# Attention values kept as two fp16 parts instead of three bf16 parts and one fp16 part

## The chip, the cores and the metric

The kernel runs on one core of one Trainium2 chip. A core has five engines that run beside each other: TensorE (PE, matrix products; its weight loads are listed apart as PEld), VectorE (DVE), ScalarE (ACT), GpSimd (POOL) and SyncE (SP), which here only issues DMAs. Products land in PSUM, 8 banks of 128 x 512 fp32; everything else works from SBUF. The metric is the time of one execution on the device, in microseconds; lower is better. The kernel was timed in three runs.

## The reference

A modulated layer norm, attention with 32 heads of 16 columns over 2048 rows of 512, and then a mixing block with its own layer norms, four weight matrices and two gelus. Everything is fp32 and a single sequence.

```python
h = _layernorm(x) * (1 + ca) + sa
q, k, v = split(h @ wqkv)                       # 32 heads x 16
scores = einsum("bhqd,bhkd->bhqk", q, k) * 16 ** -0.5
p = softmax(scores)
x = x + ga * (einsum("bhqk,bhkd->bhqd", p, v) @ wo)
h = _layernorm(x) * (1 + cb) + sb
x1 = h + shift(gelu(_layernorm(h) @ w1)) @ w2
x = x + gb * (x1 + gelu(_layernorm(x1) @ w3) @ w4)
```

## The kernel before

**Precision.** PE works on numbers with short mantissas, so each fp32 matrix is split into a high and a low part and a product is made of three (helper `mm3`, lines 339, 341 and 343, which every projection uses). The probabilities P are kept as integers: the exponential (line 1017) writes int32, scaled by 2^26. The upper 16 bits of each integer are read in place as fp16 numbers; the lower 16 bits are turned into fp16 by `p_low` (lines 1057 to 1073), on POOL as a rule (L1072) and in two halves on ACT when POOL lags (it shows as L127 in the profile). v is kept so that P times v keeps its digits: three bf16 parts of 16 columns each (offsets 0, VD = 20 and 2 VD = 40 of the 64 columns that belong to a head), a column of ones beside the first part, which yields the softmax's denominator, and a fourth copy in fp16, scaled down by VHI, for the lower halves of P. A tile row of v has 192 two-byte numbers for two heads: 128 for the three parts (`v_hi`), 64 for the fp16 copy (`v_lo`). `v_weights` scales each column of v's weights by a bound on that column, so that v stays under VMAX; the scale is put back in wo.

**Making v.** `v_tiles` runs over 16 row tiles for each half of the heads, 32 tiles in all. A tile is 12 matmuls into a bank, then a chain: ACT copies the first part (L770), ACT the fp16 copy (L771), DVE subtracts the first part from the bank into an fp32 tile vr (L751), ACT copies the second part from vr (L773), POOL subtracts that from vr for the third part (L774), and a store to DRAM follows (Vs). At most three tiles are alive (`vlive`) and at most two use vr (`vrs`). For the first half the part that unit 0 needs also goes straight to the tile vst.

**Attention.** A unit is two heads and a chunk of 512 queries; there are 64 units of 16 steps (a step s is 128 keys), 1024 steps in all. For each step PE makes two score blocks (L1021), ACT their exponentials (L1017), POOL the lower halves (L1072), and PE the products with v: `pv_part` has four matmuls for the upper halves (L1098, 32 columns of v each, two for each head) and, once for two steps, four and four for the lower halves (L1095). All of them add up in one bank. Row maxima are taken 24 steps ahead: PE makes the scores the other way round (L1005), DVE reduces them (L1001), and the shift goes into the query tile through small DMAs. At a unit's end ACT copies the bank (`ac_copy`), PE transposes it (L1127), DVE sums the parts (L1134, `sums`), takes the reciprocal of the denominator (L1144), and POOL multiplies (L1138, `fin`).

**Order.** All engines' queues are written in advance by a planner in the kernel (`Sched`). It keeps a modelled time for each engine; attention is the main line and everything else is filler, dealt out between its blocks by a budget. `sch.chain` queues the steps of a chain with a modelled cost each; `sch.dma` (line 101) charges each DMA to a modelled SP queue, with its bytes divided by 360 per ns and at least 475 ns. Its count of bytes per element is line 103:

```python
n = 2 if o.dtype == BF16 else 4
```

Filler in time order: v for heads 0 to 15, keys, v for heads 16 to 31, keys, queries, meanwhile the splitting of the other weights into 40 half pieces (`pieces_load`, `pieces_gen`; loads to the tiles wst, results stored to Ws by way of three tiles wq). The rest of the network for a chunk of 512 rows is `tail(ci)`; its weights come back from Ws. The first tail may start once all keys, values, queries and pieces are done, at step 248 at the earliest (constant TPO); from step 264 on (TPL) the program waits for them by force. The last tail runs after attention has ended.

Of the kernel before, what the change touches and what calls it, by code (L numbers as in the profile page):

```python
# [8 lines left out]
F32 = mybir.dt.float32  # L9
F32R = mybir.dt.float32r  # L10
BF16 = mybir.dt.bfloat16
F16 = mybir.dt.float16
I32 = mybir.dt.int32
U16 = mybir.dt.uint16
AF = mybir.ActivationFunctionType
OP = mybir.AluOpType
AX = mybir.AxisListType
# [3 lines left out]
S, D, H, DH, F = 2048, 512, 32, 16, 1792  # L21
P = 128
KT = D // P
NKT = S // P
# [6 lines left out]
GELU_C = 0.7978845608028654  # L31
PBITS = 26
PEXP = PBITS * 0.6931471805599453
VHI = 2.0 ** 39
VMAX = 2.0 ** 14
VD = 20

SC0 = (32, 900.0, 700.0)
TAILB = (0.0, 500.0, 560.0, 590.0)
# [24 lines left out]
NV = 3  # L64
# [233 lines left out]
def cA(n=CH):  # L298
    return n / 1.2 + 52
# [6 lines left out]
def cG(n=CH):  # L306
    return 2.2 * n + 40
# [3 lines left out]
def kernel(ctx, tc, A_x, A_wqkv, A_wo, B_w1, B_w2, B_w3, B_w4, c, w_mod, out):  # L311
# [46 lines left out]
        return t[:, :, 0:128].rearrange("p a (b n) -> p a b n", b=2)  # L358

    def v_lo(t):  # L360
        return t[:, :, 128:192].bitcast(F16).rearrange("p a (b n) -> p a b n", b=2)


    ident = con.tile([P, P], F32, name="ident")
# [13 lines left out]

    Qs = dr.tile([H * DH, 3, S], F32, name="Qs")
    Ks = dr.tile([H * DH, 3, S], F32, name="Ks")  # L380
    Vs = dr.tile([NP, P, NKT, 192], BF16, name="Vs")
    FG = [(0, 4), (4, 4), (8, 4), (12, 2)]
    pieces = []
    order = {"wo": [], "w1": [], "w2": [], "w3": [], "w4": []}
# [88 lines left out]

    kst, qtl = [], []

    zero = con.tile([4, CH], F32, name="zero")
    pool.memset(zero, 0.0)

    def unit_tiles(pl, i, e, e2):
# [234 lines left out]

    vt = []
    for i in range(NV):
        t = qp.tile([P, H // 4, 192], BF16, name=f"vt{i}")
        pool.memset(t, 0.0)
        pool.memset(v_hi(t)[:, :, :, DH:DH + 1], VHI)
        pool.memset(v_lo(t)[:, :, :, 8 + DH:9 + DH], 1.0)  # L720
        vt.append(t)

    def v_gen(w, a):
# [2 lines left out]
        yield lambda: not vlive  # L726
        done.add(("v", a))

    vlive, vrs = [], [0]
    direct, near = [], set()  # L730

    def v_tiles(w, a, kts):
        wh, wl = halves(w, KT)
        for kt in kts:
            ci, t = divmod(kt, TPC)
            h = hT[ci]
            yield lambda: len(vlive) < NV and vrs[0] < 2 and sch.room() and ("hT", ci) in done
            vrs[0] += 1
            vlive.append(kt)
            b = dbank("v")[:, :256]  # L740
            for k in range(KT):
                for _ in mm3(b, h[:, k, 0, t * P:(t + 1) * P], h[:, k, 1, t * P:(t + 1) * P],
                             wh[:, k], wl[:, k], k == 0, k == KT - 1):
                    yield nsq(256)
            w = vt[kt % NV]
            v, vl = v_hi(w), v_lo(w)
            b3 = b.rearrange("p (a b d) -> p a b d", b=2, d=DH)
            r = qp.tile([P, H // 4, 2, DH], F32, name="vr", tag="vr", bufs=2)

            def rest(v=v, b3=b3, r=r, b=b):  # L750
                dve.tensor_tensor(r, b3, v[:, :, :, 0:DH], op=OP.subtract)  # L751
                sch.free(b)

            def store(kt=kt, w=w):
                vrs[0] -= 1

                if not a and direct:
                    sch.dma(dma.dma_start, direct[kt // 4][:, kt % 4], w[:, 0])
                    near.add(kt)

                def gone():
                    vlive.remove(kt)
                    done.add(("vk", a, kt))
                    if kt % 4 == 3:
                        done.add(("v", a, kt // 4))
                e = sch.dma(dma.dma_start, Vs[8 * a:8 * a + 8, :, kt, :].rearrange("a p n -> p a n"),
                            w)
                sch.after(e, gone)

            sch.chain(("A", cA(256), lambda v=v, b3=b3: act.activation(v[:, :, :, 0:DH], b3, AF.Copy)),  # L770
                      ("A", cA(256), lambda vl=vl, b3=b3: act.activation(vl[:, :, :, 8:8 + DH], b3, AF.Copy, scale=1.0 / VHI)),  # L771
                      ("D", cD(256), rest),
                      ("A", cA(256), lambda v=v, r=r: act.activation(v[:, :, :, VD:VD + DH], r, AF.Copy)),  # L773
                      ("G", cG(256), lambda v=v, r=r: pool.tensor_tensor(v[:, :, :, 2 * VD:2 * VD + DH], r, v[:, :, :, VD:VD + DH],  # L774
                                                                         op=OP.subtract)),
                      (None, 0, store), prio=VP, bank=b)

    def v_weights(a):
# [175 lines left out]

    unit_tiles(at, 1, pool, pool)
    qst, mxs, osb = {}, {}, {}
    vst = [at.tile([P, NKT // 4, 192], BF16, name=f"vst{i}") for i in range(4)]
    direct += vst
    pv, pt = {}, {}
    pts = [at.tile([P, 2, CH], I32, name=f"pt{i}") for i in range(NPT)]  # L960
# [1 line left out]
    def load_unit(u):  # L962
        ci, pr = units[u]
        qst[u] = q = qtl[u % 3]
        cs = slice(ci * CH, (ci + 1) * CH)
        load_rows(q, Qs, pr, cs, slice(0, CH))
        if u > 2:
            sch.dma(dma.dma_start, q[0::32].bitcast(F32), zero)
        load_rows(kst[u % 3], Ks, pr, slice(0, S), slice(0, S))

    vnext = set()
# [85 lines left out]
    def p_low(s):  # L1057

        p = pt[s].rearrange("p j n -> p (j n)")
        o, i = p.bitcast(F16)[:, 0::2], p.bitcast(U16)[:, 0::2]  # L1060
        ready = e_exp.pop(s) + XX
        g, a = [max(sch.T[e], ready) for e in "GA"]
        if g > a + LACT:

            def half(h):
                c = slice(h * CH, (h + 1) * CH)
                e_low[s] = XP["A"] + sch.crit("A", 690, ready, partial(act.activation, o[:, c], i[:, c], AF.Copy, scale=0.5))
            half(0)
            e_low[s] += 690 + 480
            second.append(partial(half, 1))  # L1070
        else:
            e_low[s] = XP["G"] + sch.crit("G", 1345, ready, lambda: pool.tensor_scalar(  # L1072
                o, i, 0.5, 1.0, op0=OP.mult, op1=OP.mult))

    def pv_ready(s, lo):

# [2 lines left out]
    def pv_part(s, lo):  # L1079


        u, kt = divmod(s, NKT)
        if kt == 0 and not lo:
            pv[u] = ap_.tile([P, CH], F32, name="pv", tag="v", bufs=1)
        load_v(u, kt // 4) if (u, kt // 4) in vnext else None
        v, acc = vst[kt // 4], pv[u]

        def mms():
            for j in range(2):
                for i in range(2):  # L1090
                    r = 64 * j + 32 * i
                    if lo:
                        n = 9 + DH if i else 1 + DH
                        c = 128 + 32 * j + 9 + DH
                        te.matmul(acc[r:r + n, :], v[:, (kt + i) % 4, c - n:c].bitcast(F16), pt[s + i].bitcast(F16)[:, j, 0::2],  # L1095
                                  start=False, stop=kt == NKT - 2, skip_group_check=True)
                    else:
                        te.matmul(acc[r:r + 32, :], v[:, kt % 4, r:r + 32], pt[s].bitcast(F16)[:, j, 1::2],  # L1098
                                  start=kt == 0, stop=False, skip_group_check=True)
        e = sch.put("P", CCOL, 0.0, mms)  # L1100
        if lo:
            for i in range(2):
                pts.append(pt.pop(s + i))
                e_low.pop(s + i)
            if kt % 4 == 2:
                if u + 1 < NU:
                    vnext.add((u + 1, kt // 4))
                sch.after(e + VLATE, partial(load_v, u + 1, kt // 4))
            if kt == NKT - 2:
                acs.append((u, e + COUT))  # L1110
# [9 lines left out]
    def o_fin(u, ac, ready):  # L1120
        ci, pr = units[u]
        if pr == 0:
            osb[ci] = at.tile([P, TPC, D], F32, name="osb", tag="osb", bufs=1)
        yield lambda: sch.T["P"] >= ready and sch.room()
        b = dbank("ot")
        for t in range(TPC):
            te.transpose(b[:, t * P:(t + 1) * P], ac[:, t * P:(t + 1) * P], ident)  # L1127
            yield 110
        bv = b.rearrange("p (th n) -> p th n", n=64)
        sm = at.tile([P, 8, DH + 1], F32, name="sm", tag="sm", bufs=1)  # L1130
        rc = at.tile([P, 8, 1], F32, name="rc", tag="rc", bufs=2)

        def sums():
            dve.reduce_sum(sm, bv[:, :, 0:3 * VD].rearrange("p th (a d) -> p th d a", a=3)[:, :, 0:DH + 1, :], axis=AX.X)  # L1134
            sch.free(b)

        def fin():
            pool.tensor_tensor(osb[ci][:, :, pr * 32:pr * 32 + 32].rearrange("p t (h d) -> p t h d", d=DH),  # L1138
                              sm[:, :, 0:DH].rearrange("p (t h) d -> p t h d", h=2),
                              rc.rearrange("p (t h) o -> p t h o", h=2).to_broadcast([P, TPC, 2, DH]), op=OP.mult)  # L1140
            if pr == NP - 5:
                sch.add(tail(ci), 0 if ci == NC - 1 else None)

        sch.chain(("D", 490, sums), ("D", 90, lambda: dve.reciprocal(rc, sm[:, :, DH:DH + 1])), ("G", 350, fin),  # L1144
                  *([mark(("att", ci))] if pr == NP - 1 else []), prio=0, bank=b)


# [555 lines left out]
```

## Time and profile before

| what | us |
|---|---|
| median of 3 runs | 1999.7 |
| the runs | 1993.77, 1999.7, 2000.05 |
| span of the profiled execution (the page gives no other time of it) | 2000.7 |
| PE busy in it | 1920.9 |
| DVE, ACT, POOL busy | 1652.2, 1473.6, 1676.1 |
| first score matmuls of attention, last product with v | about 98, 1846 |

Each engine's row on the page gives busy time, share of the span and instructions. A group of instructions is named by line, engine, operation, output <- input, shapes and count; behind the first bar stand total busy us and mean ns, behind the second the idle time of the engine just before and what ended it. Rows that begin with a stretch (206.00:330.00) give an engine's busy time in it, with the number of its instructions. A wait "A <- B: 91.4, 221, 3.8" says that A waited for B for 91.4 us in all, 221 times, 3.8 us at the longest.

### The profile page before, as it was taken

Reading aid. Unit: us, or ns where it says so; the run is one execution under the profiler, and the core shown is the slowest. Engines: PE = TensorE matmul, PEld = TensorE weight load, DVE = VectorE, ACT = ScalarE, POOL = GpSimd, SP = SyncE. Lnnn points to the kernel's source line nnn. Section 1 sums busy time; section 2 is a strip of 40 time slices with the busy share of each in tenths; the row PEclk is TensorE's granted clock in tenths of the full one; section 3 lists DMA queues with packets and bytes.
Section 4 is the critical chain, followed back from the end, with each engine's and each line's share of the span. In section 5 each row is a group of like instructions: output and inputs, shape, how many; then the busy total and the mean of one; then the engine's idle time right before and its main releaser. Section 6 shows DMA issues by size and latency. Waiting matters only on the chain.

```text
span 2000.7 us, 42354 instructions
## 1 busy us (share of the span) xinstructions
PE 1920.9 (96%) x14480; PEld 1146.7 (57%) x14480; DVE 1652.2 (83%) x3010; ACT 1473.6 (74%) x3083; POOL 1676.1 (84%) x1609
## 2 busy tenths in 40 slices
PE   7999999999999999999999999999999999999899
PEld 4655555555455555555455555555555555555798
DVE  7887988888899888888989898898898889883643
ACT  5376888777878777777878787786787878777443
POOL 6287999889999998888999998898899989888532
PEclk8999999999999999999999999999999999999999
DMA  5767677766643334345433333334433343334432
GB/s 184 205 201 228 182 231 218 244 225 192 198 157 111 115 103 143 109 136 162 126 111 92 109 111 114 115 119 148 157 98 100 115 151 107 121 95 147 149 146 90
DMA packets 232352, 293.24 MB, mean 147 GB/s; under 512 B 125876, under 2 KB 177076, under 8 KB 215848
## 3 DMA queue, kind: packets, MB, share of 16 engines
q1 hardware_dynamic: 232136, 290.53, 46.4%
q8 instruction: 115, 1.88, 0.4%
q14 instruction: 101, 0.83, 0.1%
HBM read 225.81 MB, written 62.91 MB: 144 GB/s over the span
## 4 chain that ended last, share of the span: by engine, by line
PE 67%; DVE 16%; ACT 8%; issue 3%; POOL 2%; DMA 2%; SPq 1%; POOLq 0%; ACTq 0%; DVEq 0%
PE mb L1005 14%; PE sc L1021 10%; PE pv L1098 10%; DVE mx L1001 9%; PE w L339 7%; PE w L343 6%; PE w L341 6%; PE pv L1095 4%; ACT pt L1017 4%; POOL pt L1072 2%; DVE xs L1421 1%; DVE sq L1418 1%; DMA vst<-Vs 1%; PE mr L644 1%; PE ot L1127 1%
## 5 line engine op out<-in xcount | busy, mean ns | idle before, releaser
L1072 POOL TENSOR_SCALAR pt<-pt 128x1024 f16<-128x1024 uint16 x988 | 1312.5, 1365 | 132.6 <-ACT pt L1017 125.4
L1001 DVE TENSOR_REDUCE mx<-mb 128x1 f32<-128x512 f32 x2048 | 1281.0, 683 | 76.0 <-PE mb L1005 54.5
L1017 ACT ACTIVATE pt<-sc 128x512 int32<-128x512 f32 x2048 | 1090.8, 606 | 272.3 <-PE mb L1005 164.9
L1005 PE MATMUL mb<-kst,qtl 64*128 64x512 f32 x2048 | 752.1, 454 | 49.0 <-ACT pt L1017 16.1
L1021 PE MATMUL sc<-qtl,kst 64*128 64x512 f32 x2048 | 716.4, 444 | 2.6 <-DVE A L329 0.6
L1005 PEld LDWEIGHTS mb<-kst,qtl 64*128 64x128 f32 x2048 | 348.7, 193 | 254.5 <-DVE mx L1001 91.4
L1021 PEld LDWEIGHTS sc<-qtl,kst 64*128 64x128 f32 x2048 | 335.6, 186 | 153.5 <-DVE mx L1001 47.1
L1098 PE MATMUL pv<-pt,vst 128*32 128x512 f16 x4096 | 358.2, 397 | 0.1
L1095 PE MATMUL pv<-pt,vst 128*17 128x512 f16 (+1 forms) x2048 | 213.7, 394 | 2.2 <-POOL pt L1072 1.7
L1098 PEld LDWEIGHTS <-vst 128*32 128x32 bf16 x4096 | 90.9, 95 | 167.6 <-issue 108.8
L339 PE MATMUL w<-A,wr 128*128 128x256 f32 (+2 forms) x576 | 175.3, 304 | 0.3 <-ACT A L333 0.3
L1428 POOL TENSOR_TENSOR g<-xs,g 128x256 fp32r<-128x256 f32 (+2 forms) x144 | 103.2, 718 | 83.4 <-ACT g L1427 81.3
L341 PE MATMUL w<-A,wr 128*128 128x256 f32 (+2 forms) x576 | 169.8, 295 | 0.5 <-DVE A L329 0.3
L343 PE MATMUL w<-A,wr 128*128 128x256 f32 (+2 forms) x576 | 167.7, 291 | 0.0
L339 PEld LDWEIGHTS w<-A,wr 128*128 128x128 f32 x576 | 109.6, 190 | 35.4 <-DVE mx L1001 10.3
L339 PE MATMUL w<-wr,g 128*128 128x512 f32 x288 | 119.2, 414 | 0.6 <-ACT g L1427 0.6
L341 PEld LDWEIGHTS w<-A,wr 128*128 128x128 f32 x576 | 109.9, 191 | 12.4 <-issue 11.3
L343 PE MATMUL w<-wr,g 128*128 128x512 f32 x288 | 114.7, 398 | 0.2 <-POOL g L1428 0.2
L341 PE MATMUL w<-wr,g 128*128 128x512 f32 x288 | 113.6, 394 | 0.0
L343 PEld LDWEIGHTS w<-A,wr 128*128 128x128 f32 x576 | 109.8, 191 | 6.7 <-issue 6.7
L1535 DVE TENSOR_TENSOR x<-x,w 128x512 f32<-128x512 f32 x64 | 43.9, 687 | 82.0 <-PE w L343 82.0
L1424 ACT ACTIVATE sq<-w 128x256 f32<-128x256 f32 (+2 forms) x144 | 55.7, 387 | 68.8 <-PE w L343 66.0
(151 smaller groups left out, 2103.8 us busy)
## 6 DMA issues: line engine op xcount, KB each, us to landing
wr<-Ws SPq DMA_DIRECT2D x80, 1024.0 KB
kst<-Ks SPq DMA_DIRECT2D x189, 256.0 KB
vst<-Vs SPq DMA_DIRECT2D x252, 192.0 KB
qtl<-Qs SPq DMA_DIRECT2D x192, 64.0 KB
Vs<-vt SPq DMA_DIRECT2D x32, 384.0 KB
Ws<-wq SPq DMA_DIRECT2D x40, 256.0 KB
Ws<-wst SPq DMA_DIRECT2D x40, 256.0 KB
wst<-in_B_w_dram SPq DMA_DIRECT2D x36, 256.0 KB
```

The costliest lines, as they stand in the source:

```text
L339: te.matmul(o, lh, rh, start=first, stop=False)
L341: te.matmul(o, lh, rl, start=False, stop=False)
L343: te.matmul(o, ll, rh, start=False, stop=last)
L1001: end = sch.crit("D", 605, e + PX, lambda: dve.reduce_max(mxs[u][:, j, g, c:c + 1], b, axis=AX.X))
L1005: return ready, lambda: te.matmul(b, lhs, kst[u % 3][r, c * CH:(c + 1) * CH], start=True, stop=True), after
L1017: ea = sch.crit("A", 480, e + PX, lambda: act.activation(pt[s][:, j], b, AF.Exp))
L1021: return ready, lambda: te.matmul(b, kst[u % 3][r, kt * P:(kt + 1) * P], qst[u][r], start=True, stop=True), after
L1072: e_low[s] = XP["G"] + sch.crit("G", 1345, ready, lambda: pool.tensor_scalar(o, i, 0.5, 1.0, op0=OP.mult, op1=OP.mult))
L1095: te.matmul(acc[r:r + n, :], v[:, (kt + i) % 4, c - n:c].bitcast(F16), pt[s + i].bitcast(F16)[:, j, 0::2], start=False, stop=kt == NKT - 2 ...
L1098: te.matmul(acc[r:r + 32, :], v[:, kt % 4, r:r + 32], pt[s].bitcast(F16)[:, j, 1::2], start=kt == 0, stop=False, skip_group_check=True)
L1424: sch.chain(("A", cA(n), lambda: act.activation(sq, b, AF.Square)), ("D", cD(n), cube), ("A", cA(n), lambda: act.activation(sq, sq, AF.Tan ...
L1428: ("G", cG(n), lambda: pool.tensor_tensor(lo, xs, hi, op=OP.subtract)), (None, 0, end), bank=b)
```

## The change

v is kept as two fp16 parts (offsets 0 and VD = 32) with the column of ones scaled to 2^15, and one further fp16 copy of the first part scaled by 2^-20, for the lower halves of P, which are scaled by 2^-20 instead of 0.5. The second part is written by the DVE subtraction itself; the fp32 tile vr, the second ACT copy and the POOL subtraction are gone, and with them the limit of two tiles on vr. The lower halves' matmuls all have 17 columns (before, 17 and 25). The sum at a unit's end runs over two parts, its planned cost is 360 ns instead of 490, and its tiles have two and three buffers instead of one and two. The tile of zeros is 4 x 128 instead of 4 x 512 and is read four times over by the DMA. The tiles of v are of type F16 instead of BF16; line 103 is as it was.

```diff
-VHI = 2.0 ** 39
-VMAX = 2.0 ** 14
-VD = 20
+VHI = 2.0 ** 15
+VMAX = 1.0
+VLO = 2.0 ** -20
+PLO = 2.0 ** -20
+VD = 32
...
-        return t[:, :, 128:192].bitcast(F16).rearrange("p a (b n) -> p a b n", b=2)
+        return t[:, :, 128:192].rearrange("p a (b n) -> p a b n", b=2)
...
-    Vs = dr.tile([NP, P, NKT, 192], BF16, name="Vs")
+    Vs = dr.tile([NP, P, NKT, 192], F16, name="Vs")
...
-    zero = con.tile([4, CH], F32, name="zero")
+    zero = con.tile([4, P], F32, name="zero")
...
-        t = qp.tile([P, H // 4, 192], BF16, name=f"vt{i}")
+        t = qp.tile([P, H // 4, 192], F16, name=f"vt{i}")
         pool.memset(t, 0.0)
         pool.memset(v_hi(t)[:, :, :, DH:DH + 1], VHI)
-        pool.memset(v_lo(t)[:, :, :, 8 + DH:9 + DH], 1.0)
+        pool.memset(v_lo(t)[:, :, :, DH:DH + 1], VHI * VLO)
...
-            yield lambda: len(vlive) < NV and vrs[0] < 2 and sch.room() and ("hT", ci) in done
-            vrs[0] += 1
+            yield lambda: len(vlive) < NV and sch.room() and ("hT", ci) in done
...
-                dve.tensor_tensor(r, b3, v[:, :, :, 0:DH], op=OP.subtract)
+                dve.tensor_tensor(v[:, :, :, VD:VD + DH], b3, v[:, :, :, 0:DH], op=OP.subtract)
...
-                      ("A", cA(256), lambda vl=vl, b3=b3: act.activation(vl[:, :, :, 8:8 + DH], b3, AF.Copy, scale=1.0 / VHI)),
+                      ("A", cA(256), lambda vl=vl, b3=b3: act.activation(vl[:, :, :, 0:DH], b3, AF.Copy, scale=VLO)),
                       ("D", cD(256), rest),
-                      ("A", cA(256), lambda v=v, r=r: act.activation(v[:, :, :, VD:VD + DH], r, AF.Copy)),
-                      ("G", cG(256), lambda v=v, r=r: pool.tensor_tensor(v[:, :, :, 2 * VD:2 * VD + DH], r, v[:, :, :, VD:VD + DH],
-                                                                         op=OP.subtract)),
...
-    vst = [at.tile([P, NKT // 4, 192], BF16, name=f"vst{i}") for i in range(4)]
+    vst = [at.tile([P, NKT // 4, 192], F16, name=f"vst{i}") for i in range(4)]
...
-            sch.dma(dma.dma_start, q[0::32].bitcast(F32), zero)
+            sch.dma(dma.dma_start, q[0::32].bitcast(F32).rearrange("r (a n) -> r a n", n=P),
+                    zero[:, None, :].to_broadcast([4, CH // P, P]))
...
-                o, i, 0.5, 1.0, op0=OP.mult, op1=OP.mult))
+                o, i, PLO, 1.0, op0=OP.mult, op1=OP.mult))
...
-                        n = 9 + DH if i else 1 + DH
-                        c = 128 + 32 * j + 9 + DH
-                        te.matmul(acc[r:r + n, :], v[:, (kt + i) % 4, c - n:c].bitcast(F16), pt[s + i].bitcast(F16)[:, j, 0::2],
+                        n = DH + 1
+                        c = 128 + 32 * j
+                        te.matmul(acc[r:r + n, :], v[:, (kt + i) % 4, c:c + n], pt[s + i].bitcast(F16)[:, j, 0::2],
...
-        sm = at.tile([P, 8, DH + 1], F32, name="sm", tag="sm", bufs=1)
-        rc = at.tile([P, 8, 1], F32, name="rc", tag="rc", bufs=2)
+        sm = at.tile([P, 8, DH + 1], F32, name="sm", tag="sm", bufs=2)
+        rc = at.tile([P, 8, 1], F32, name="rc", tag="rc", bufs=3)
...
-            dve.reduce_sum(sm, bv[:, :, 0:3 * VD].rearrange("p th (a d) -> p th d a", a=3)[:, :, 0:DH + 1, :], axis=AX.X)
+            dve.reduce_sum(sm, bv[:, :, 0:2 * VD].rearrange("p th (a d) -> p th d a", a=2)[:, :, 0:DH + 1, :], axis=AX.X)
...
-        sch.chain(("D", 490, sums), ("D", 90, lambda: dve.reciprocal(rc, sm[:, :, DH:DH + 1])), ("G", 350, fin),
+        sch.chain(("D", 360, sums), ("D", 90, lambda: dve.reciprocal(rc, sm[:, :, DH:DH + 1])), ("G", 350, fin),
```

More of the change, by code (lines that the diff above doesn't have):

```diff
@@ L727, in v_gen @@
         done.add(("v", a))
-    vlive, vrs = [], [0]
+    vlive = []
     direct, near = [], set()
@@ L747, in v_tiles, with rest @@
             b3 = b.rearrange("p (a b d) -> p a b d", b=2, d=DH)
-            r = qp.tile([P, H // 4, 2, DH], F32, name="vr", tag="vr", bufs=2)
-            def rest(v=v, b3=b3, r=r, b=b):
-                dve.tensor_tensor(r, b3, v[:, :, :, 0:DH], op=OP.subtract)
+            def rest(v=v, b3=b3, b=b):
+                dve.tensor_tensor(v[:, :, :, VD:VD + DH], b3, v[:, :, :, 0:DH], op=OP.subtract)
                 sch.free(b)
             def store(kt=kt, w=w):
-                vrs[0] -= 1
                 if not a and direct:
@@ L1066, in half @@
                 c = slice(h * CH, (h + 1) * CH)
-                e_low[s] = XP["A"] + sch.crit("A", 690, ready, partial(act.activation, o[:, c], i[:, c], AF.Copy, scale=0.5))
+                e_low[s] = XP["A"] + sch.crit("A", 690, ready, partial(act.activation, o[:, c], i[:, c], AF.Copy, scale=PLO))
             half(0)
```

## The prediction

> **What bounds the kernel now.** I read the page first (busy time, chain of waits), then the busy time by stage, then the waits, then the lines that the change touches.
>
> ```profile
> span 2000.7 us, 42354 instructions
> PE 1920.9 (96%) x14480; PEld 1146.7 (57%) x14480; DVE 1652.2 (83%) x3010; ACT 1473.6 (74%) x3083; POOL 1676.1 (84%) x1609
> ...
> PE 67%; DVE 16%; ACT 8%; issue 3%; POOL 2%; DMA 2%; SPq 1%; POOLq 0%; ACTq 0%; DVEq 0%
> ```
>
> The page gives no time of the profiled execution beside its span, 2000.7 us. That is 1.0 us over the median of the runs, 1999.7, and the three runs spread over 6.3 us. TensorE (PE) is first: 96% busy and 67% of the chain that ended last. VectorE (DVE) holds 16% of that chain, ScalarE (ACT) 8%, GpSimd (POOL) only 2%, although POOL is busy 84% of the span.
>
> ```profile
> 206.00:330.00 124.00, 120.62 (x1029) 70.89 (x1029) 106.98 (x195) 112.28 (x246) 118.64 (x108) 1.00 0.74 212
> ...
> 50.00:1850.00 1800.00, 1744.45 (x13561) 999.50 (x13561) 1540.94 (x2782) 1387.84 (x2913) 1584.88 (x1477) 0.99 0.48 147
> ```
>
> These rows of the busy time by stage give PE, PEld, DVE, ACT, POOL, clock and DMA. From 50 to 1850 us PE idles 56 us in 1800 and DVE is busy 86%. From 206 to 330 us, where the second half of v is made, POOL is 96% and ACT 91% busy, yet PE idles only 3.4 us in 124.
>
> ```profile
> PEld mb L1005 <- DVE mx L1001: 91.4, 221, 3.8
> PEld sc L1021 <- DVE mx L1001: 47.1, 114, 1.0
> PE mb L1005 <- ACT pt L1017: 16.1, 43, 1.0
> PE mb L1005 <- DVE mx L1001: 14.5, 32, 3.5
> PEld mb L1005 <- DVE sm L1134: 9.9, 25, 0.5
> ```
>
> The waits say what PE lacks when it does wait: PSUM banks that DVE (the row maximum, L1001) or ACT (the exponential, L1017) still hold. The last row belongs to the change: 25 of 64 times the weight load waits for the summing of a unit's output, L1134.
>
> **The change part by part.**
>
> ```profile
> L1001 DVE TENSOR_REDUCE mx<-mb 128x1 f32<-128x512 f32 x2048 | 1281.0, 683 | 76.0 <-PE mb L1005 54.5 <-PE sc L1021 15.4
> L1134 DVE TENSOR_REDUCE sm<-ot 128x136 f32<-128x408 f32 x64 | 36.8, 575 | 5.4 <-PE ot L1127 5.4
> L774 POOL TENSOR_TENSOR vt<-vr,vt 128x256 bf16<-128x256 f32 x32 | 22.6, 708 | 35.3 <-ACT vt L773 25.9 <-DMA qtl<-nm 5.3 <-DMA Vs<-vt 3.5
> L773 ACT ACTIVATE vt<-vr 128x256 bf16<-128x256 f32 x32 | 13.8, 432 | 6.4 <-DVE vr L751 6.4
> L751 DVE TENSOR_TENSOR vr<-v,vt 128x256 f32<-128x256 f32 x32 | 13.5, 421 | 14.1 <-ACT vt L771 7.6 <-PE sc L1021 2.9 <-POOL pt L1072 2.2
> ...
> 206.00:330.00 124.00, 6.73 (x16) 17.52 (x48) 11.36 (x16) 1.00 0.74 212
> ```
>
> *The sums (two parts instead of three).* L1134 reads 8 x 17 x 2 = 272 elements instead of 8 x 17 x 3 = 408. The two reductions give the slope: (683 - 575) / (512 - 408) = 1.04 ns per element, so 575 - 136 x 1.04 = 434 ns, 141 less, and 64 x 141 = 9.0 us of DVE. On the path: by the chain's 16% it would be 1.4 us; by the 25 releases of the weight load, 25 x 0.141 = 3.5 us. I take 2.5. The bounds are 0 (every us hidden behind PE) and 9.0.
>
> *Making v (L770 to L774).* Each of 32 tiles loses one ACT pass (432 ns) and one POOL subtraction (708 ns): 13.8 us of ACT, 22.6 us of POOL. The DVE subtraction stays and writes fp16 straight into the tile; it still reads fp32 from PSUM, so I leave its 421 ns. Half of this work falls before 130 us, where POOL waits for these very tiles (25.9 us idle before L774), so it is worth nothing there. The last row, the busy time from 206 to 330 us on the v tile alone (DVE, ACT, POOL), holds the other 16 tiles. There POOL sheds its 11.4 us and ACT 16 x 0.432 = 6.9, but PE has just 3.4 us to give back. I take 1.0; the bounds are 0 and 3.4.
>
> ```profile
> L1098 PE MATMUL pv<-pt,vst 128*32 128x512 f16 x4096 | 358.2, 397 | 0.1
> L1095 PE MATMUL pv<-pt,vst 128*17 128x512 f16 x1024 | 210.6, 394 | 0.5 <-POOL pt L1072 0.5
> L1095 PE MATMUL pv<-pt,vst 128*25 128x512 f16 x1024 | 208.0, 394 | 1.7 <-POOL pt L1072 1.1 <-ACT pt L127 0.4
> L1095 PEld LDWEIGHTS <-vst 128*25 128x25 f16 x1024 | 53.1, 94 | 1.6 <-issue 1.0
> L1095 PEld LDWEIGHTS <-vst 128*17 128x17 f16 x1024 | 52.1, 91 | 48.6 <-issue 7.4
> ...
> L1072 POOL TENSOR_SCALAR pt<-pt 128x1024 f16<-128x1024 uint16 x988 | 1312.5, 1365 | 132.6 <-ACT pt L1017 125.4 <-ACT mf L1052 1.7 <-POOL pt L1072 1.1
> ```
>
> *P times v.* The same 6144 matmuls with the same 512 columns. L1095 already has an fp16 stationary operand and takes 394 ns against 397 for bf16 in L1098: type and width (17, 25, 32) do not set the time. 1024 weight loads shrink from 25 to 17 columns, 94 to 91 ns, four of them side by side: 1024 x 3 / 4 = 0.8 us at most, taken as 0. Dropping the third part saves no matmul, since the 64 columns of a head were two loads of 32 before and still are. The factor in L1072 and L127 is an immediate; nothing moves. For data that alter an engine's speed no row speaks; I bound it by 0.
>
> *Buffers and zeros.* sm gets two buffers, rc three: nothing in the waits shows a wait for them, so 0. The zero rows go from one run of 2 KB to four of 512 B, with the same bytes. SP carries them between other loads, and its long waits are for PE, not for itself.
>
> ```profile
> L106 SPq DMA_DIRECT2D qtl<-zero x61: 548/549/637, 131.2 to 1768.0; - x61
> SPq L106 <- PE pv L1095: 298.6, 85, 10.5
> vst<-Vs SPq DMA_DIRECT2D x252, 192.0 KB
> Vs<-vt SPq DMA_DIRECT2D x32, 384.0 KB
> ```
>
> The nearest dearer row is none for this pattern; 61 x 549 ns doubled would be 33 us of a queue that waits 298.6 us for PE alone. I take 0.
>
> *The planner's clock.* Line 103 counts 2 bytes only for BF16. With F16 tiles a 192 KB load of v is charged 1.09 us instead of 0.55, a 384 KB store 2.18 instead of 1.09, while the real transfers are unchanged. Together with the cheaper chains and the 360 for 490 in the sums' cost, this lets the planner deal its filler work out anew. I give this 0 and price its two ends under the rivals.
>
> Sum: 2000.7 - 2.5 - 1.0 = 1997.2 for the profiled execution, and 1.0 less against the median: 1996.2. I say **1996.5**, within what a measurement of this kernel can tell from no change (0.3%, 6 us).
>
> **The rivals.**
>
> *Faster: a stall falls out.*
>
> ```profile
> 341.83 6.69 DVE L901 TENSOR_TENSOR wst<-wst,wq 128x512 fp32r<-128x512 f32 x1
> ...
> 340.00:350.00 10.00, 6.32 (x38) 3.50 (x27) 10.00 (x8) 4.64 (x9) 8.03 (x7) 0.96 0.43 134
> 350.00:360.00 10.00, 9.78 (x68) 4.43 (x72) 8.74 (x15) 6.64 (x13) 6.47 (x6) 0.70 0.59 186
> 450.00:460.00 10.00, 9.52 (x37) 5.21 (x36) 5.57 (x10) 4.80 (x11) 8.87 (x7) 0.66 0.79 252
> ...
> L1535 DVE TENSOR_TENSOR x<-x,w x64: 677/687/690, 771.7 to 1997.1; 128x512 f32<-128x512 f32 x64
> ```
>
> At 341.8 us one DVE subtraction with both operands in SBUF took 6.69 us; the same size with one operand in PSUM (L1535) never took over 0.69. POOL ran without a pause meanwhile. PE lost 3.7 us in that slice, and in the next its clock fell to 0.70, 3.0 us more. Elsewhere the clock falls too (0.66 at 450 us). The Trainium skill, "GPSIMD Engine Reference", section Specifications, says that POOL shares its SBUF interfaces with DVE instructions that have two SBUF inputs; the trace agrees, 6.69 us against 0.69. With less POOL work and another order this stall may go: 3.7 + 3.0 on top of the 3.5 gives 1996.2 - 6.7 = **1989.5**. Against it: a new order can also make one, which would put the time near 2003 (one) or 2009 (two).
>
> By the Trainium skill, "TensorE: Matmul & The Clock Gate", Part 1, the clock has only half and full rate, chosen over a free-running window of 3.4 us. By that rule a dip costs an estimated 1.7 us per window and moves with the phase of the run; 0.70 and 0.66 over 10 us fit two windows.
>
> *Slower: the planner's dearer DMAs hold the weights back.*
>
> ```profile
> 520.00:560.00 40.00, 0.00 (x0) 0.00 (x0) 1.00 0.43 131
> ...
> 960.00:1000.00 40.00, 0.00 (x0) 0.00 (x0) 1.00 0.48 149
> ...
> 104.00:520.00 416.00, 163.36 (x458) 76.48 (x458) 0.98 0.72 221
> 520.00:546.00 26.00, 13.93 (x38) 6.30 (x38) 1.00 0.39 119
> ...
> L106 SPq DMA_DIRECT2D Ws<-wst x40: 319/392/1375, 152.2 to 543.7; - x40
> ```
>
> The first two rows count L339 (the first product of each projection), the next two the score matmuls, L1021: from 520 to 560 us there is no filler, because the tail may start only when all 40 half pieces of the weights are stored (last at 543.7 us) and score step 248 is reached (38 score matmuls in 26 us there, about 545 us). If pieces come later, up to step 264, 32 score matmuls or 22 us on, nothing is lost: the first tail has 40 us of slack at 960. Past that the program drains and PE stands still, us for us. Three work tiles pass 40 pieces in 543.7 - 152.2 = 391 us, so one piece takes about 29 us and passes SP's planned queue twice. A planned lag of 0.8 us per pass makes 40 x 2 x 0.8 / 3 = 21 us, the point from which it decides; 1.2 us gives 32 us, 10 over, so **2006.5**. For it: worked from the code's costs, the planned queue is charged some 98 of the 124 us from 206 to 330 and 125 after (a unit of 32 score matmuls lasts 416 / 458 x 32 = 29 us, so 4.3 units x 2.2 us and 16 stores x 1.1 us more). Against it: POOL gives back 11.4 us in the same stage, and pieces wait mostly for POOL and ACT.
>
> *The change does not do what it says* would be fp16 weights running at another rate; L1095 against L1098 excludes it, so it has no chance of its own.
>
> **How the numbers follow.** Forecast (1994 to 2005.5): 0.47. Stall gone or savings passed on in full: 0.36, faster. Late weights: 0.11, slower; a new stall or two: 0.06, slower. So faster 0.36, within 0.3% 0.47, slower 0.17. The bounds of the sums (0 and 9.0 us) and of v (0 and 3.4) give 1987.3 to 1999.7; with the stall gone as well the best is 1980.6, at a low chance. I set the range to 1985 and 2007: about 0.07 below, 0.12 above.
>
> **What would show it.** Right: L1134 near 434 ns; L773 and L774 gone and L751 still near 421; L1098 at 397 with an fp16 load; waits for L1134 shorter; PE busy time unchanged. Wrong: POOL's relief turning into more than 3.4 us between 206 and 330 us; the filler gap that begins at 520 us lasting past 590 us, or a PE stall behind it; the number of clock dips and of long L901 or L440 changed by more than two; L1072 off 1365 ns.

## The result and the profile after

| kernel | median, us | lowest to highest | runs |
|---|---|---|---|
| before | 1999.88 | 1993.77 to 2001.24 | 4 |
| after | 2076.85 | 2072.42 to 2079.44 | 4 |

The changed kernel takes 1.0388 times as long (interval 1.0371 to 1.0405): 77 us slower. The forecast was 1996.5 us, no change that can be measured, with a range that ended at 2007. The prediction was wrong, by far more than its range allowed.

From the page of the changed kernel, the span, the busy times and the chain that ended last:

```profile
span 2074.4 us, 42389 instructions
PE 1944.9 (94%) x14480; PEld 1154.8 (56%) x14480; DVE 1647.5 (79%) x3010; ACT 1463.2 (71%) x3043; POOL 1720.2 (83%) x1581
PE 59%; POOL 15%; DVE 12%; ACT 7%; issue 4%; DMA 2%; SPq 1%; POOLq 0%; ACTq 0%; DVEq 0%
```

GpSimd's share of the chain went from 2% to 15%, TensorE's from 67% to 59%. POOL has 28 instructions fewer than before (1581 for 1609) and is busy 44 us longer. The groups by line and shape of the changed kernel, as before the bar busy us and mean ns, behind it the idle time just before:

```profile
L1068 POOL TENSOR_SCALAR pt<-pt 128x1024 f16<-128x1024 uint16 x992 | 1348.8, 1360 | 153.7 <-ACT pt L1013 77.5 <-POOL pt L1068 0.2
L1130 DVE TENSOR_REDUCE sm<-ot 128x136 f32<-128x272 f32 x64 | 27.6, 432 | 3.3 <-PE ot L1123 3.2
L751 DVE TENSOR_TENSOR vt<-v,vt 128x256 f16<-128x256 f32 x32 | 13.4, 420 | 15.9 <-ACT vt L769 13.5 <-PE sc L1017 2.4
L1094 PE MATMUL pv<-pt,vst 128*32 128x512 f16 x4096 | 363.4, 398 | 0.0
L1091 PE MATMUL pv<-pt,vst 128*17 128x512 f16 x2048 | 233.4, 395 | 39.2 <-POOL pt L1068 37.7 <-ACT pt L129 1.2
```

Four of the five are as forecast: the sums at 432 ns (434 forecast), the subtraction of v at 420 (421), the matmuls of P times v at 398 and 395. The first, the lower halves on POOL (L1072 before, L1068 here), looks innocent too: 1360 ns for 1365. But the last row shows PE waiting 37.7 us for it, where before it waited 1.7 (1.1 and 0.5 in the rows of L1095). In the waits of the changed kernel POOL in turn waits less for its input, the exponentials, 77.5 us against 125.4:

```profile
POOL pt L1068 <- ACT pt L1013: 77.5, 54, 12.5
PE pv L1091 <- POOL pt L1068: 37.7, 49, 2.5
```

So POOL has become late, with instructions that are no longer than they were. The timeline of POOL solves this. Its columns are start, duration and the instruction; neighbours of one line are drawn together, with their count at the end. First the kernel before, then the changed one, at the same place of attention:

```profile
1062.56 0.64 POOL L1428 TENSOR_TENSOR g<-xs,g 128x256 fp32r<-128x256 f32 x1
1063.17 7.81 POOL L1072 TENSOR_SCALAR pt<-pt 128x1024 f16<-128x1024 uint16 x6
1070.90 0.64 POOL L1428 TENSOR_TENSOR g<-xs,g 128x256 fp32r<-128x256 f32 x1
```

```profile
1084.38 4.19 POOL L1068 TENSOR_SCALAR pt<-pt 128x1024 f16<-128x1024 uint16 x3
1088.64 0.55 POOL L1320 TENSOR_TENSOR trs<-tmv,mhalf 128x1 f32<-128x1 f32 x1
```

Before, six instructions of 1.36 us end after 7.81 us: (7.81 - 1.36) / 5 = 1.29 us from start to start, so each begins 0.07 us before its neighbour has ended. The next one, L1428, begins at 1070.90, also before 1063.17 + 7.81 = 1070.98. After, three end after 4.19 us: (4.19 - 1.36) / 2 = 1.42 us from start to start, and the next begins 0.07 us after the end of the last. Over all groups of neighbours from 600 to 1800 us, the medians for groups of 2 to 5 give steps of 1.29 to 1.31 us before and 1.43 to 1.45 after; I use 1.295 and 1.437. The duration in the row is the same; what a lower half takes from POOL rose by 0.142 us, an estimate of 992 x 0.142 = 141 us of POOL.

There is a second loss. The half pieces of the weights come late; the row of their last store gives count, shortest, median and longest ns, and the first and last start:

```profile
L108 SPq DMA_DIRECT2D Ws<-wst x40: 319/394/1552, 151.9 to 590.8; - x40
```

The last is stored at 590.8 us instead of 543.7, and PE is busy 46.21 of the 60 us from 540 to 600, where it was 58.18.

### The profile page after: what moved, and what is told of

Same layout as the page of the kernel before. It is cut to its first block, busy times and chain, and to the rows that moved or that the text cites. A ratio compares the mean times of both kernels' runs of the same rounds, so it can differ in the third digit from the quotient of the medians.

```text
span 2074.4 us, 42389 instructions
## 1 busy us (share of the span) xinstructions
PE 1944.9 (94%) x14480; PEld 1154.8 (56%) x14480; DVE 1647.5 (79%) x3010; ACT 1463.2 (71%) x3043; POOL 1720.2 (83%) x1581
## 4 chain that ended last, share of the span: by engine, by line
PE 59%; POOL 15%; DVE 12%; ACT 7%; issue 4%; DMA 2%; SPq 1%; POOLq 0%; ACTq 0%; DVEq 0%
PE mb L1001 12%; POOL pt L1068 11%; PE sc L1017 9%; PE pv L1094 8%; DVE mx L997 6%; PE w L341 6%; PE w L345 6%; PE w L343 6%; PE pv L1091 4%; ACT pt L1013 4%; PE ot L1123 1%; SPq L108 1%; DVE xs L1417 1%; PE mr L646 1%; POOL g L1424 1%
## 5 line engine op out<-in xcount | busy, mean ns | idle before, releaser
L1068 POOL TENSOR_SCALAR pt<-pt 128x1024 f16<-128x1024 uint16 x992 | 1348.8, 1360 | 153.7 <-ACT pt L1013 77.5
L1094 PE MATMUL pv<-pt,vst 128*32 128x512 f16 x4096 | 363.4, 398 | 0.0
L1091 PE MATMUL pv<-pt,vst 128*17 128x512 f16 x2048 | 233.4, 395 | 39.2 <-POOL pt L1068 37.7
L1094 PEld LDWEIGHTS <-vst 128*32 128x32 f16 x4096 | 91.4, 95 | 168.2 <-issue 112.8
L341 PE MATMUL w<-A,wr 128*128 128x256 f32 (+2 forms) x576 | 176.4, 306 | 0.6 <-ACT A L335 0.6
L341 PEld LDWEIGHTS w<-A,wr 128*128 128x128 f32 x576 | 110.4, 192 | 34.6 <-ACT pt L1013 9.4
L1091 PEld LDWEIGHTS <-vst 128*17 128x17 f16 x2048 | 60.8, 91 | 114.8 <-issue 72.8
L341 PE MATMUL w<-wr,g 128*128 128x512 f32 x288 | 118.4, 411 | 0.6 <-ACT g L1423 0.6
```

What stands on the lines that cost most here:

```text
L341: te.matmul(o, lh, rh, start=first, stop=False)
L1091: te.matmul(acc[r:r + n, :], v[:, (kt + i) % 4, c:c + n], pt[s + i].bitcast(F16)[:, j, 0::2], start=False, stop=kt == NKT - 2, skip_group_ ...
```

## The experiments

Two edits of the change were suspected: the factor on the lower halves (0.5 became 2^-20) and the planner's charge for DMAs of v (4 bytes an element where it was 2). The first four kernels take each edit out of the changed kernel, and put each alone into the kernel before. E1, E2 and E6 below give the lower halves another weight in the result (too large by 2^19, too small by 2^19, too large by 2^19), but leave no work out.

**E1: the changed kernel with the old factor.** Lines 1063 (ACT) and 1069 (POOL):

```diff
-                o, i, PLO, 1.0, op0=OP.mult, op1=OP.mult))
+                o, i, 0.5, 1.0, op0=OP.mult, op1=OP.mult))
```

> The changed kernel with the lower halves of P scaled by 0.5 as before, on POOL and on ACT; order and planner untouched. It changes what is computed: the lower halves of P count 2^19 times too much. Theory 1 (the scaling instruction on POOL holds the engine longer when it scales by 2^-20: in the trace runs of them step by 1.437 us instead of 1.295, though each row still says 1.36): the step goes back to 1.30 and the time to 1995 to 2015 us. Theory 2 (the planner, which charges fp16 DMAs double, has dealt out a worse order): the step may change, the time stays within 2060 to 2080.

2018.02 us (2016.93 to 2021.44), kernel before 1997.67, ratio 1.0101 (1.0074 to 1.0128). The step of POOL is 1.295 us again, POOL has 3% of the chain, and POOL waits 143.6 us for the exponentials instead of 77.5. The factor alone accounts for 2076.85 - 2018.02 = 59 us. Some 20 us remain.

**E2: the kernel before with the new factor.** The same two lines the other way round, 0.5 to 2^-20.

> The kernel before with the lower halves of P scaled by 2^-20 instead of 0.5, nothing else; the lower halves then count 2^19 times too little. Theory 1: step 1.44 us, time 2050 to 2085. Theory 2: 1994 to 2006, as before.

2057.79 us, ratio 1.0297 (1.0270 to 1.0324): 60 us from one constant (in two lines, POOL's and ACT's), with nothing else of the change in the kernel. The step is 1.438 us. From the timeline of POOL and the waits of this kernel:

```profile
1089.50 8.52 POOL L1072 TENSOR_SCALAR pt<-pt 128x1024 f16<-128x1024 uint16 x6
```

```profile
PE pv L1095 <- POOL pt L1072: 35.8, 48, 2.4
```

Six take 8.52 us where the kernel before has six in 7.81, and PE's wait for POOL appears.

**E3: the changed kernel with 2 bytes charged for fp16.**

```diff
-        n = 2 if o.dtype == BF16 else 4
+        n = 2 if o.dtype in (BF16, F16) else 4
```

> The changed kernel with line 105 counting 2 bytes for F16 too, so the planner charges the v transfers as it did before. The last weight piece is then stored in the order after unit 16's shifts, as before, instead of unit 18's. Theory 1: the step stays 1.44 and the time 2055 to 2080. Theory 2: 1990 to 2010.

2061.85 us, ratio 1.0317 (1.0290 to 1.0343): 15 us less than the changed kernel. The step stays 1.438, the last piece is stored at 547.8 us.

**E4: the kernel before with 4 bytes charged for everything.**

```diff
-        n = 2 if o.dtype == BF16 else 4
+        n = 4
```

> The kernel before with 4 bytes charged for every DMA, the same real transfers. Theory 1: 1992 to 2010, whatever the order does. Theory 2: 2040 or more.

2021.93 us (2019.02 to 2024.48), ratio 1.0119 (1.0086 to 1.0152): 24 us slower, between what the two theories had expected, so both sizes were wrong. The step is 1.295; the pieces are not late (last store at 543.0 us). The 24 us are lost elsewhere. The first copies of v's tiles between 190 and 420 us, for the kernel before and then for E4, begin and end at:

```profile
L770 ACT ACTIVATE vt<-v x16: 384/384/422, 206.3 to 324.1; 128x256 bf16<-128x256 f32 x16
```

```profile
L770 ACT ACTIVATE vt<-v x16: 383/383/394, 250.1 to 356.4; 128x256 bf16<-128x256 f32 x16
```

The second half of v starts 44 us later and ends 32 us later. The chain that ended last, in E4 (start, duration, what):

```profile
361.05 0.44 SPq L106
361.55 0.59 SPq L106
...
365.87 3.04 DMA wst<-in_B_w_dram
368.99 0.64 ACT wst L899
369.65 0.63 ACT wq L900
370.28 0.49 ACT pt L1017
370.82 0.79 PE mb L1005
```

A load of a weight piece stands in SP's queue behind stores and shifts and is issued at 365.87 us. ACT has the instruction that uses it (L899) queued ahead of an exponential, and PE waits for that exponential: in the timeline of PE, the bracket is the idle time before the instruction and what ended it.

```profile
370.82 0.79 PE L1005 MATMUL mb<-kst,qtl 64*128 64x512 f32 x1 [10.22 <-ACT pt L1017]
```

That one wait is 10.2 of the 24 us. Counting score matmuls by time shows that the loss is made before 400 us: E4 has 8 fewer than the kernel before at 300 us, 26 fewer at 400, and 17 fewer at 1800 (0.9 us each).

**E5: the same number in two factors.** Why would a constant cost time? One theory (A) was small results: an integer under 2^16 times 2^-20 is often under 2^-14, where fp16 has only its subnormal numbers. The other (B) was the factor itself, as it is written in the instruction. 2^-10 times 2^-10 gives the same results with other factors.

```diff
-                o, i, PLO, 1.0, op0=OP.mult, op1=OP.mult))
+                o, i, 2.0 ** -10, 2.0 ** -10, op0=OP.mult, op1=OP.mult))
```

> The changed kernel with the factor 2^-20 on POOL given as 2^-10 times 2^-10 (two immediates instead of 2^-20 and 1): the same numbers come out. Theory A (the step is long because results fall among the fp16 subnormals, below 2^-14: lower halves under 64 do): step 1.44 us, time 2070 to 2082. Theory B (it is the immediate 2^-20 itself): step 1.30, time 2010 to 2025.

2014.61 us in one run (kernel before 1998.89), step 1.295. The results are the same small numbers, and the loss is gone: the theory of small results falls. ACT's factor is still 2^-20 here, so it is POOL's that costs. In the timeline of POOL of E5 four take (5.21 - 1.36) / 3 = 1.28 us from start to start:

```profile
1079.19 5.21 POOL L1068 TENSOR_SCALAR pt<-pt 128x1024 f16<-128x1024 uint16 x4
```

**E6: a small factor, ordinary results.** The reverse: 2^-20 and then 2^19 on POOL, 0.5 on ACT.

```diff
-                o, i, PLO, 1.0, op0=OP.mult, op1=OP.mult))
+                o, i, 2.0 ** -20, 2.0 ** 19, op0=OP.mult, op1=OP.mult))
```

> The changed kernel with the POOL factors 2^-20 and then 2^19, so that 0.5 times the lower half comes out (ACT's halves scaled by 0.5 too; the lower halves of P count 2^19 times too much). Theory A: step 1.30, time 2012 to 2025. Theory B: step 1.44, time 2070 to 2082.

2076.31 us in one run, step 1.438, and PE waits 35.6 us for POOL. The results are those of E1, the time is that of the changed kernel. It is the factor.

**E7 and E8: 2^-14 instead of 2^-20**, with the fp16 copy of v scaled by 2^-26 to match; E8 also has the edit of E3.

```diff
-VLO = 2.0 ** -20
-PLO = 2.0 ** -20
+VLO = 2.0 ** -26
+PLO = 2.0 ** -14
```

> The changed kernel with the lower halves scaled by 2^-14 and the fp16 copy of v by 2^-26 (their product is as in the change, and no scaled lower half but zero lies below 2^-14, the smallest normal fp16 number). Theory A: step 1.30, time 2012 to 2025. Theory B: step 1.44 if any small power of two does it, time 2070 to 2082.

> As the run before, with line 105 counting 2 bytes for F16 too: what is left of the change when both costs are taken away. Theory A with the planner's part as measured (15 us in the changed kernel, 24 in the one before): 1993 to 2008. Theory B: 2055 to 2068.

E7: 2078.18 us, ratio 1.0395 (1.0364 to 1.0426), step 1.44. E8: 2063.97, ratio 1.0323 (1.0298 to 1.0348), step 1.437. 2^-14 is as dear as 2^-20, and both kernels agree with those of 2^-20 (2076.85 and 2061.85). No lower half but zero lies under the fp16 normal range here, so theory A fails this test too.

**E9: both costs taken away**, the edits of E3 and E5 together. Everything else of the change is in it, with the same numbers computed.

> The changed kernel, results unchanged, with both costs taken away: the POOL factor given as 2^-10 times 2^-10, and line 105 counting 2 bytes for F16. If the immediate and the planner's charge are all that the change lost: 1996 to 2003, the forecast of the prediction (1996.5); if something else of the change costs time too: 2005 or more; if the savings come through: under 1994.

1999.83 us (1996.28 to 2007.23, 12 runs) against 1998.47 (17 runs of the kernel before): ratio 1.0010 (0.9992 to 1.0028). No change: the interval is -1.6 to +5.6 us. So the factor and the charge are the whole loss, within these few us, and what is left of the change is worth nothing that could be measured. From the groups by line of E9, and its busy time from 206 to 330 us:

```profile
L751 DVE TENSOR_TENSOR vt<-v,vt 128x256 f16<-128x256 f32 x32 | 13.4, 418 | 11.5 <-ACT vt L769 7.7 <-PE sc L1017 2.8 <-PE mb L1001 1.0
L1130 DVE TENSOR_REDUCE sm<-ot 128x136 f32<-128x272 f32 x64 | 27.5, 429 | 3.0 <-PE ot L1123 3.0
```

```profile
206.00:330.00 124.00, 122.35 (x1054) 73.07 (x1056) 108.35 (x194) 106.58 (x226) 118.96 (x100) 1.00 0.81 233
```

**E10: which factors cost.** Twelve pairs of factors in one kernel, each with the product 2^-20 and a line of its own (1069 to 1080), dealt out by the step's number modulo 12; the first, fourth, fifth and sixth are

```diff
+                lambda: pool.tensor_scalar(o, i, 2.0 ** 0, 2.0 ** -20, op0=OP.mult, op1=OP.mult),
...
+                lambda: pool.tensor_scalar(o, i, 2.0 ** -10, 2.0 ** -10, op0=OP.mult, op1=OP.mult),
+                lambda: pool.tensor_scalar(o, i, 2.0 ** -11, 2.0 ** -9, op0=OP.mult, op1=OP.mult),
+                lambda: pool.tensor_scalar(o, i, 2.0 ** -12, 2.0 ** -8, op0=OP.mult, op1=OP.mult),
```

> The changed kernel, results unchanged, with twelve pairs of POOL factors in turn, all with the product 2^-20: (1, 2^-20), (2^-1, 2^-19), (2^-6, 2^-14), (2^-10, 2^-10), (2^-11, 2^-9), (2^-12, 2^-8), (2^-13, 2^-7), (2^-14, 2^-6), (2^-17, 2^-3), (2^-20, 1), (2^4, 2^-24), (2^-24, 2^4), each on a line of its own. If a small first immediate is what costs, the gap after an instruction is there from one of the lines on, between 2^-11 and 2^-14, and the rest has none; if a small immediate in either place costs, the first three and the eleventh have it too; if the value of the immediate is not it, all or none have it.

2054.18 us in one run. From the timeline of POOL; L1071 is (2^-6, 2^-14), L1072 (2^-10, 2^-10), L1073 (2^-11, 2^-9), L1074 (2^-12, 2^-8):

```profile
1125.23 1.36 POOL L1071 TENSOR_SCALAR pt<-pt 128x1024 f16<-128x1024 uint16 x1
1126.67 1.36 POOL L1072 TENSOR_SCALAR pt<-pt 128x1024 f16<-128x1024 uint16 x1
1127.95 1.36 POOL L1073 TENSOR_SCALAR pt<-pt 128x1024 f16<-128x1024 uint16 x1
1129.39 1.38 POOL L1074 TENSOR_SCALAR pt<-pt 128x1024 f16<-128x1024 uint16 x1
```

From start to start: 1.44, 1.28, 1.44. Among neighbouring lower halves the pairs L1072 to L1073 overlap (the median of 58 is 0.07 us), and so does the only pair of L1070 and L1072; the others have a gap of 0.08 us. By itself that looks like a bound: the two lines have no factor under 2^-11. But here each line has nearly always the same neighbours, and one slow instruction is enough to lose the overlap, before or behind it. So a quick line between two slow ones can't be told from them. The neighbours of other kinds tell them apart (L1070 is (2^-1, 2^-19), L1077 (2^-17, 2^-3), L1078 (2^-20, 1), L1437 a subtraction of the tail):

```profile
694.87 1.38 POOL L1070 TENSOR_SCALAR pt<-pt 128x1024 f16<-128x1024 uint16 x1
696.18 0.64 POOL L1437 TENSOR_TENSOR g<-xs,g 128x256 fp32r<-128x256 f32 x1
696.91 1.36 POOL L1071 TENSOR_SCALAR pt<-pt 128x1024 f16<-128x1024 uint16 x1
698.35 0.64 POOL L1437 TENSOR_TENSOR g<-xs,g 128x256 fp32r<-128x256 f32 x1
```

```profile
687.08 1.37 POOL L1077 TENSOR_SCALAR pt<-pt 128x1024 f16<-128x1024 uint16 x1
688.37 0.65 POOL L1437 TENSOR_TENSOR g<-xs,g 128x256 fp32r<-128x256 f32 x1
689.11 1.38 POOL L1078 TENSOR_SCALAR pt<-pt 128x1024 f16<-128x1024 uint16 x1
```

L1437 begins 0.07 us before the end of L1070 and 0.08 us before that of L1077, but 0.08 us after that of L1071. Over the whole trace, the time from a lower half's end to the start of a following instruction of another line, as medians (a minus is an overlap; idle times over 0.15 us are not counted):

| pair | us, times | pair | us, times |
|---|---|---|---|
| (1, 2^-20) | 0.08, 32 | (2^-13, 2^-7) | 0.08, 27 |
| (2^-1, 2^-19) | -0.07, 17 | (2^-14, 2^-6) | 0.08, 16 |
| (2^-6, 2^-14) | 0.08, 31 | (2^-17, 2^-3) | -0.07, 33 |
| (2^-10, 2^-10) | -0.07, 18 | (2^-20, 1) | 0.08, 19 |
| (2^-11, 2^-9) | -0.08, 36 | (2^4, 2^-24) | 0.08, 30 |
| (2^-12, 2^-8) | 0.08, 15 | (2^-24, 2^4) | 0.08, 13 |

Four pairs are quick without an exception, and two of them have a factor of 2^-17 or 2^-19. None of the three outcomes that I had named fits, and there is no bound under which a factor is dear: the value counts, but not by its size. The total fits roughly. Of the 1216 transitions in the trace that touch a lower half 948 have the gap, which gives 2014.6 + 0.78 x 62 = 2063 us; it was 2054, and a single run doesn't say why.

**E11 and E12: two of the pairs alone.** The changed kernel with one pair for all: (2^-11, 2^-9) and (2^-12, 2^-8). Both expectations still take the row of neighbouring lower halves for a bound between 2^-11 and 2^-12.

```diff
-                o, i, PLO, 1.0, op0=OP.mult, op1=OP.mult))
+                o, i, 2.0 ** -11, 2.0 ** -9, op0=OP.mult, op1=OP.mult))
```

> The changed kernel with the lower halves' factor given as 2^-11 times 2^-9, nothing else changed. Theory B with its bound (a factor of 2^-12 or smaller on either place of the instruction costs 0.14 us, one of 2^-11 does not): start-to-start step of lower-half instructions 1.295 us, time 2010 to 2022 us. Rival (only the pair of 2^-10 was ever seen alone as quick, 2^-11 may be past the bound when all instructions have it): step 1.437, time 2070 to 2082.

> The changed kernel with the factor given as 2^-12 times 2^-8, nothing else changed. Theory B with its bound: step 1.437 us, time 2070 to 2082 us. Rival (the bound lies lower, between 2^-12 and 2^-14, and the gap in the mixed kernel came from the neighbour's factors): step 1.295, time 2010 to 2022.

One run each, beside 2003.17 for the kernel before: 2021.39 us with a step of 1.295, and 2076.03 us with a step of 1.437. The timelines of POOL, E11 and then E12:

```profile
1082.65 7.76 POOL L1068 TENSOR_SCALAR pt<-pt 128x1024 f16<-128x1024 uint16 x6
```

```profile
1084.62 4.18 POOL L1068 TENSOR_SCALAR pt<-pt 128x1024 f16<-128x1024 uint16 x3
```

Each pair alone is as quick or as slow as it was among the twelve, and between these two lie 55 us of this kernel. The bound that the two expectations speak of would fit these two runs, but not (2^-1, 2^-19) and (2^-17, 2^-3) of E10.

| | charge as before | dearer charge |
|---|---|---|
| step 1.295 us | before 1999.9, E9 1999.8 | E4 2021.9, E1 2018.0, E5 2014.6, E11 2021.4 |
| step 1.437 us | E2 2057.8, E3 2061.9, E8 2064.0 | after 2076.9, E6 2076.3, E7 2078.2, E12 2076.0 |

The table puts the medians of the kernels together (E5, E6, E11 and E12 are single runs; the kernel before, measured beside each group, had medians of 1997.7 to 2003.2). Between kernels that are alike in the other one of the two costs, the factor costs 55 to 64 us down a column, and the charge 14 to 24 along a row.

## Why the prediction was wrong

**The step that failed: "The factor in L1072 and L127 is an immediate; nothing moves. For data that alter an engine's speed no row speaks; I bound it by 0."** That term was 59 to 62 us (E1 against the changed kernel, E2 against the kernel before, E3 against E9). A bound of 0 on one side only, for an edit to 992 instructions of an engine that is busy 96% in one stage, was no bound. The profile before couldn't give the price. It could give what each 0.1 us on L1072 is worth: 988 x 0.1 = 99 us of POOL, against 125.4 us that POOL waits for exponentials, with PE right behind. So the edit deserved a rival of its own.

**Where the time on POOL went.** The 141 us leave out the neighbours of other lines, which lose their overlap too. Counted in the traces of E1 and of the changed kernel, POOL's busy time with the gaps up to 0.15 us rose from 1673.9 to 1828.7 us, by 155. Its longer idle times fell by 97 us (335.5 to 238.4), 66 of them in front of L1068, where POOL waited 143.6 us for exponentials in E1 and 77.5 after. The other 58 are what the span grew by (2016.6 to 2074.4).

**What would have shown it wrong was itself wrong.** I named "L1072 off 1365 ns" as the sign. The row says 1360, 5 ns shorter, and in E2, where nothing else was changed, 1360 too. The time between one end and the next start is what changed. The Trainium skill, "Perfetto Trace Analysis", section GPSIMD Engine Instruction, says that a GpSimd span in a profile is unreliable and that one should time by the start-to-start spacing of consecutive instructions. The runs agree: 1360 and 1365 ns for steps of 1.437 and 1.295 us. Another sign did come: from 540 to 600 us no first product of a projection (L341 here) runs in the changed kernel, so the filler gap lasted past 590 us.

**The rival "the planner's dearer DMAs hold the weights back" happened**, at a chance of 0.11. Its price was 2006.5, 10 us over the forecast; it measured 15 (E3 against after) to 24 us (E4 against before). Its mechanism was half right. In the changed kernel the last piece is stored at 590.8 us (E1 575.9, before 543.7) and PE loses 12.0 us of the 60 from 540 to 600 (E1, with 50.00 busy, 8.2). PE, by 20 us, in the changed kernel:

```profile
540.00:560.00 20.00, 16.36 (x130) 1.00 0.62 190
560.00:580.00 20.00, 15.48 (x118) 1.00 0.61 186
580.00:600.00 20.00, 14.37 (x102) 0.83 0.50 163
600.00:620.00 20.00, 19.21 (x134) 1.00 0.59 220
```

But there are two dates, and I had seen one. The second half of v has a date as well: unit 8 is the first of the upper heads, at about 98 + 8 x 29 = 330 us. E4, whose v is stored 36 us later (366.4 for 330.6), loses its time there, with its pieces in time. That this date is what crowds the queues at 360 us is my reading of the order; no run tried it alone. And the program doesn't drain quietly: in E4's chain ACT took the late load's user (L899) before the exponential queued behind it, and PE stood for 10.2 us. "POOL gives back 11.4 us in the same stage" was the argument against; it did not help.

**What was right.** With both costs gone (E9) the durations are what the sum said, but its 3.5 us did not come: by the medians E9 is 1.4 us over the kernel before, with an interval of -1.6 to +5.6 that leaves the -3.5 just outside. L1130 took 432 (after) and 429 ns (E9) for 434; L751 at 420 and 418 for 421; matmuls at 398 and 395; L773 and L774 gone. From 206 to 330 us PE is busy 1.7 us longer in E9 (122.35 for 120.62), where I took 1.0 of at most 3.4. Not as said: the weight loads' wait for the sums did not shrink (9.9 us before, 9.7 in E9), so the 2.5 us there did not show.

**The rival "a stall falls out"** (1989.5, with 0.36 on the faster side) was no gain. The longest L901 is 6.69 us before; the same line takes at most 1.74 us in the changed kernel (L896 there) and 1.79 in E9, with POOL busy 83% of the span in both, so a busy POOL alone doesn't make such a stall. PE in E9, by 20 us from 320 to 400:

```profile
320.00:340.00 20.00, 19.87 (x148) 1.00 0.77 242
340.00:360.00 20.00, 19.84 (x149) 1.00 0.64 210
360.00:380.00 20.00, 15.70 (x98) 0.93 0.76 258
380.00:400.00 20.00, 19.26 (x131) 0.90 0.75 251
```

The hole at 340 us is closed (19.84 us busy for 16.10 before) and another opens 20 us on, where PE's small matmuls (L646) wait 4.3 us for a load. The four sum to 74.67 us; before, they summed to 75.01.

**What stays open.** Why POOL loses its overlap with some pairs of factors and not with others, no run here shows. One pattern fits all fifteen pairs that ran: quick are those whose two exponents both lie in 0 to -3, -8 to -11 or -16 to -19, that is, every second block of four, and every slow pair has one outside of these. I found it after the runs, and none of them was made to test it. Neither is it shown why E10 is quicker than its mix of steps, nor which waits make up the rest of the charge's 14 to 24 us.

## What to carry to other kernels

A constant inside an instruction can cost time: when a change rescales data, time the rescaled instruction by the spacing of its starts, and if it has become slow, try the same number as another pair of factors, if the instruction has room for two. A small factor needn't be dear and a moderate one needn't be cheap, so the pair has to be measured. An unchanged mean duration does not clear a line; look at who began to wait for it. Where a planner prices work by type, a change of type is a change of order, and every date by which filler must be done is a rival with its own price.

## What the hardware showed unexpectedly

Lower halves of 128 x 1024 on GpSimd follow each other after 1.295 us with the factors 0.5 and 1, 2^-10 twice, or 2^-11 and 2^-9, and after 1.437 us with 2^-20 and 1, 2^-20 and 2^19, 2^-14 and 1, or 2^-12 and 2^-8, with 1.36 us in the row in both cases. The size of the results plays no part (E5, E6), and the size of the factors isn't the rule: in E10 the pairs (2^-1, 2^-19) and (2^-17, 2^-3) overlap with their neighbours of other lines by 0.07 us, and (2^-6, 2^-14) leaves 0.08 us. Two lower halves overlap only if both are of a quick pair. The loss touches neighbours of other lines too: in the changed kernel L1320 begins 0.07 us after the end of L1068, in the kernel before L1428 begins 0.08 us before the end of L1072.
